# Score masks on ScalarE that take the eighth maximum itself as bias, and one VectorE operation for the exponential's bias in place of three on GpSimd

## The chip, the core and the metric

The kernel runs on one core of one Trainium2 chip. The metric is the time of one execution on the device in microseconds (us): 1217.75 as the median of three runs (1216.57 to 1219.38). Everything is computed in fp32, partly with operands split into two parts.

## The reference, cut to what matters

Attention over 4 batches and 8 heads, 576 positions, 64 channels, in which each row keeps only its 32 largest scores, and behind it two MLPs (512 to 2048 and back) over the 2304 tokens:

```python
scores = scale * np.matmul(q, k.transpose(0, 1, 3, 2))
kth = np.partition(scores, -top_k, axis=-1)[..., -top_k:-top_k + 1]      # top_k = 32
mask = scores >= kth
scores = np.where(mask, scores, -1000000000.0)
scores = scores - np.max(scores, axis=-1, keepdims=True)
attn = np.exp(scores)
attn = attn / (np.sum(attn, axis=-1, keepdims=True) + 1e-09)
x = np.matmul(attn, v)                # rows of all heads side by side: 2304 x 512
h = x @ w_in;  x = (h - np.tanh(h)) @ w_out
h = x @ w_in2; x = np.where(h > 0, h, np.exp(np.minimum(h, 0)) - 1) @ w_out2
```

## The kernel before

**Stages.** The 2304 tokens go through in six chunks of 384. Chunk 0's attention runs alone; from then on the MLPs of one chunk (two times 16 steps: a product to `h`, an activation, a gate `g`, a split of `g` into `gh` and `gl`, a second product) are interleaved with the attention of the next chunk. Behind the attention of chunk 5 only MLP steps are left. The weights come packed; in chunk 0 and during its MLPs they are unpacked by ScalarE (lines 186, 203), VectorE (line 189) and a split on ScalarE and GpSimd (line 148 and 149, tile `wp`).

**Attention.** A group is up to three tiles of 128 query rows by 576 scores (tile `s`, copied from PSUM by ScalarE, line 385). A group takes four rounds r = 0 to 3. In each round VectorE finds the eight largest values of each row (`find`, MAX8, line 406, into `vm`) and, in rounds 0 to 2, replaces them by a very low number (`drop`, MATCH_REPLACE8, line 420). The eighth value of round 3 is the row's 32nd largest score, the threshold. For most tiles VectorE then multiplies the exponential with the mask (line 427). For some it is ScalarE that makes the mask: `MASK_ACT = [3, 2, 1, 0, 0, 0]` tiles of each group in chunks 0, 1 and 2 (the last group of chunk 0, which is in a hurry, has none). These are 45 tiles in 23 groups: 7 groups with three tiles, 8 with two, 8 with one.

**The mask on ScalarE.** Prelu of `s - threshold` with the slope 3e38 for negative arguments (line 422), then the exponential of that with a bias that adds back the threshold and takes off the row's largest value (line 423). The first needs `nk`, the threshold negated, the second `b2` (named `b` in the profile), the scaled threshold plus `mb`. GpSimd makes both in three small operations (lines 412, 413, 414) of 1 to 3 columns. `mb` is the negated, scaled maximum, made by GpSimd in round 0 (line 408).

**Order.** Python code issues the work by ticks (four ticks to a group); a scheduler then sets the order of the instructions on each engine, and each engine works its queue strictly in that order, so a waiting instruction holds up all that stand behind it. TensorE's score products (lines 383, 384) use three PSUM banks, which ScalarE's copies (line 385) give back.

**GpSimd's other work** in the stretch that the change touches: the low halves of the splits, all by line 149 (`wp` 1024 columns, `kk` 576, `gl` and `xl` 384), `qs` (line 326), and `xun` (line 559), most of which read two tiles in SBUF.

Of the kernel before, what the change touches and what calls it, by code (L numbers as in the profile page):

```python
# [8 lines left out]
F32 = mybir.dt.float32  # L9
# [4 lines left out]
AF = mybir.ActivationFunctionType  # L14
ALU = mybir.AluOpType
# [3 lines left out]
P = 128  # L19
# [4 lines left out]
SCALE = 0.125  # L24
# [3 lines left out]
NF = DFF // P  # L28
FILL = -1.0e38

STEEP = 3.0e38


CHUNKS = [
# [72 lines left out]
def tile_topk_attention_two_mlps(  # L107
# [9 lines left out]
    nc = tc.nc  # L117

    def pool(name, bufs, space=None):
        kw = {} if space is None else {"space": space}  # L120
        return ctx.enter_context(tc.tile_pool(name=name, bufs=bufs, **kw))

    const = pool("const", 1)
    sb = pool("sb", 2)
# [108 lines left out]
    for ci, size in enumerate(SIZES):  # L233
        for p in range(NPAIR):
            row = []
            c0 = 0
            for b, q0, n in CHUNKS[ci]:
                for heads in ([[0], [1]] if n >= 256 else [[0, 1]]):
                    u = Unit()
# [18 lines left out]
            for us in cuts:  # L258
                g = Group()
# [11 lines left out]
    def hurried(u):  # L271

        return u.rush and u.last
# [113 lines left out]
    def topk_steps(g, r):  # L387

        k = len(g.tiles)
        if r == 0:  # L390
            g.vm = sb.tile([P, 4, 2, 8], F32, tag="vm", name=f"vm{g.id}")
            g.mb = sb.tile([P, 4], F32, tag="mb", name=f"mb{g.id}")
            g.sum = sb.tile([P, 4], F32, tag="sum", name=f"sum{g.id}", bufs=8)
            g.w = [sb.tile([P, S], F32, tag="w3", name=f"w3{g.id}_{j}", bufs=W_BUFS) for j in range(k)]
        if r == 1:
            for u in g.units:
                u.e = [sb.tile([P, S], F32, tag="e", name=f"e{u.id}_{t}", bufs=E_BUFS) for t in range(u.k)]

        by_act = 0 if g.rush and hurried(g.units[-1]) else min(k, MASK_ACT[g.units[0].ci])
        if r == 3 and by_act:  # L400
            g.nk = sb.tile([P, 4], F32, tag="nk", name=f"nk{g.id}")
            g.b2 = sb.tile([P, 4], F32, tag="b2", name=f"b2{g.id}")

        def find(j):
            u, t = g.tiles[j]
            nc.vector.max(g.vm[:, j, min(r, 1)], u.s[t] if r == 0 else g.w[j])  # L406
            if r == 0 and j == k - 1:
                nc.gpsimd.tensor_scalar_mul(g.mb[:, :k], g.vm[:, :k, 0, 0], -SCALE)
            if r == 1 and j >= by_act:
                nc.scalar.activation(u.e[t], u.s[t], AF.Exp, bias=g.mb[:, j : j + 1], scale=SCALE)  # L410
            if r == 3 and j == by_act - 1:
                nc.gpsimd.tensor_scalar_mul(g.nk[:, :by_act], g.vm[:, :by_act, 1, 7], -1.0)
                nc.gpsimd.tensor_scalar_mul(g.b2[:, :by_act], g.vm[:, :by_act, 1, 7], SCALE)
                nc.gpsimd.tensor_add(g.b2[:, :by_act], g.b2[:, :by_act], g.mb[:, :by_act])

        def drop(j):
            u, t = g.tiles[j]
            v = g.vm[:, j, min(r, 1)]
            if r < 3:
                nc.vector.match_replace(g.w[j], v, u.s[t] if r == 0 else g.w[j], FILL)  # L420
            elif j < by_act:
                nc.scalar.activation(u.e[t], u.s[t], AF.Prelu, bias=g.nk[:, j : j + 1], alpha=STEEP)
                nc.scalar.activation(  # L423
                    u.e[t], u.e[t], AF.Exp, bias=g.b2[:, j : j + 1], scale=SCALE, accum_out=g.sum[:, j : j + 1]
                )
            else:
                nc.vector.scalar_tensor_tensor(
                    u.e[t], u.s[t], v[:, 7:8], u.e[t], op0=ALU.is_ge, op1=ALU.mult, accum_out=g.sum[:, j : j + 1]
                )

        return [lambda j=j, d=d: d(j) for d in (find, drop) for j in range(k)]

    def transposed(g, blk):
# [297 lines left out]
    for tick in range(FIRST_TICK, n_ticks):  # L731
# [10 lines left out]
        for u in units:  # L742
            if hurried(u) and tick == 4 * u.g.at + 4:
# [4 lines left out]
                finish_pair(u)  # L748
        at, r = divmod(tick, 4)
        chain = topk_steps(groups[at], r) if 0 <= at < len(groups) else []  # L750
        todo = [step_parts(i) for i in at_tick.get(tick, ())]
        cuts = [len(chain) * j // (2 * max(1, len(todo))) for j in range(2 * max(1, len(todo)) + 1)]
# [60 lines left out]
```

## Time and profile before

| what | value |
|---|---|
| median of three runs | 1217.75 us |
| the profiled execution | 1221.19 us, of which the span of instructions is 1219.4 us |
| busy in the span: PE, DVE, ACT, POOL | 94%, 78%, 63%, 41% |
| granted TensorE clock, mean over the span | 0.972 |

PE is TensorE, PEld its weight loads, DVE VectorE, ACT ScalarE, POOL GpSimd. The shares of the whole span mix stages: the first 170 us are attention alone, then comes the interleaved stretch, and from 1050 us on the MLPs run alone. In the chain that ended last (it can be followed back to 451 us) PE has 58% of the span, ACT 2% and DVE 1%.

### The profile page before, as it was taken

What the parts mean: (1) busy time and instruction counts of PE and PEld (TensorE: products, weight loads), DVE (VectorE), ACT (ScalarE), POOL (GpSimd) and SP (SyncE); (2) the same over time, 40 slices, a digit from 0 to 9 for tenths busy, and PEclk for the clock granted to TensorE, in tenths of its full rate; (3) what the DMA queues carried; (4) which work ended last, traced back from release to release, by engine and by line L of the source; (5) the groups of instructions that cost most, each with busy time, mean ns of one, the idle gap of its engine ahead of it and who ended that gap; (6) DMA issues with size and microseconds to landing.
All of it is one profiled execution on the core that took longest, in us unless ns stands there. A gap on an engine that the chain in (4) does not pass through costs nothing.

```text
span 1219.4 us, 18848 instructions
## 1 busy us (share of the span) xinstructions
PE 1150.4 (94%) x6349; PEld 976.2 (80%) x6349; DVE 950.1 (78%) x1896; ACT 764.1 (63%) x1592; POOL 503.1 (41%) x557
## 2 busy tenths in 40 slices
PE   6477789998999999999999999999999999999998
PEld 3344478887887978898988988988988988898897
DVE  7899999998999999789888779898789996100111
ACT  4999978988975546474564666575555564432333
POOL 2345348666752323253524444434434413333221
PEclk9688899998999999999999999999999999999999
DMA  7999728984989985759886779988679875686572
GB/s 233 361 354 336 241 73 295 365 288 142 385 345 290 288 302 144 246 162 315 251 187 206 238 239 247 226 243 271 218 248 221 205 154 207 210 285 247 195 270 95
DMA packets 81328, 299.59 MB, mean 246 GB/s; under 512 B 18768, under 2 KB 36048, under 8 KB 51664
## 3 DMA queue, kind: packets, MB, share of 16 engines
q1 hardware_dynamic: 81232, 298.39, 76.8%
q8 instruction: 50, 0.82, 0.3%
q14 instruction: 46, 0.38, 0.1%
HBM read 252.97 MB, written 45.39 MB: 245 GB/s over the span
## 4 chain that ended last, share of the span: by engine, by line
PE 58%; ACT 2%; DVE 1%; POOL 0%; issue 0%; ACTq 0%; POOLq 0%; DVEq 0%
PE acc L613 24%; PE h L577 24%; PE av L470 3%; PE pt L448 3%; PE ps L383 2%; PE ps L384 2%; DVE vm L406 0%; ACT y L627 0%; DVE w L420 0%; ACT zh L632 0%; ACT e L410 0%; ACT ph L449 0%; ACT s L385 0%; POOL kk L149 0%; ACT t L583 0%
## 5 line engine op out<-in xcount | busy, mean ns | idle before, releaser
L149 POOL TENSOR_TENSOR gl<-g,gh 128x384 fp32r<-128x384 f32 x192 | 203.4, 1061 | 371.8 <-ACT gh L148 352.3
L406 DVE MAX8 vm<-w 128x8 f32<-128x576 f32 x432 | 315.8, 748 | 3.2
L613 PE MATMUL acc<-wt,gh 128*128 128x512 f32 x1002 | 267.2, 398 | 0.3 <-ACT gh L148 0.3
L420 DVE MATCH_REPLACE8 w<-vm,w 128x576 f32<-128x576 f32 x288 | 212.8, 740 | 0.0
L613 PEld LDWEIGHTS acc<-wt,gh 128*128 128x128 f32 x1002 | 183.7, 188 | 33.9 <-issue 2.7
L148 ACT ACTIVATE gh<-g 128x384 fp32r<-128x384 f32 x192 | 100.6, 526 | 83.8 <-DVE g L591 43.3
L591 DVE SCALAR_TENSOR_TENSOR g<-t,h 128x384 f32<-128x384 f32 x96 | 52.4, 545 | 127.8 <-ACT t L583 127.4
L577 PE MATMUL h<-zh,wt 128*128 128x384 f32 (+2 forms) x768 | 145.8, 326 | 2.4 <-ACT zh L632 1.2
L613 PE MATMUL acc<-wt,gl 128*128 128x512 f32 x501 | 146.4, 398 | 0.0
L577 PE MATMUL h<-xh,wt 128*128 128x384 f32 x664 | 140.0, 339 | 2.0 <-DVE g L591 1.2
L448 PE MATMUL pt<-ident,e 128*116 128x128 f32 (+1 forms) x720 | 117.8, 290 | 20.2 <-ACT e L423 8.3
L385 ACT ACTIVATE s<-ps 128x288 f32<-128x288 f32 (+1 forms) x272 | 106.8, 416 | 45.2 <-PE ps L384 36.6
L406 DVE MAX8 vm<-s 128x8 f32<-128x576 f32 x144 | 107.4, 751 | 34.6 <-ACT s L385 32.6
L577 PEld LDWEIGHTS h<-zh,wt 128*128 128x128 f32 x768 | 124.9, 190 | 8.8 <-ACT zh L632 2.4
L449 ACT ACTIVATE ph<-pt 116x384 f32<-116x384 f32 (+1 forms) x240 | 111.2, 500 | 30.0 <-PE pt L448 29.5
L448 PEld LDWEIGHTS pt<-ident,e 128*116 128x116 f32 (+1 forms) x720 | 90.4, 143 | 43.2 <-ACT e L423 11.4
L577 PEld LDWEIGHTS h<-xh,wt 128*128 128x128 f32 x664 | 116.2, 188 | 9.0 <-DVE g L591 1.5
L582 ACT ACTIVATE t<-h 128x384 f32<-128x384 f32 x96 | 46.7, 488 | 108.2 <-PE h L577 108.0
L613 PEld LDWEIGHTS acc<-wt,gl 128*128 128x128 f32 x501 | 92.1, 188 | 18.5
L420 DVE MATCH_REPLACE8 w<-vm,s 128x576 f32<-128x576 f32 x144 | 106.6, 741 | 0.0
L580 ACT ACTIVATE t<-h 128x384 f32<-128x384 f32 x96 | 47.0, 491 | 90.9 <-PE h L577 90.8
L596 DVE TENSOR_TENSOR g<-h,t 128x384 f32<-128x384 f32 x76 | 41.4, 546 | 72.0 <-ACT t L580 71.5
(82 smaller groups left out, 1958.3 us busy)
## 6 DMA issues: line engine op xcount, KB each, us to landing
wt<-w SPq DMA_DIRECT2D x167, 1024.0 KB, 6.0
wr<-in_w_dram SPq DMA_DIRECT2D x32, 1024.0 KB, 8.9
w<-wp SPq DMA_DIRECT2D x32, 1024.0 KB, 8.4
kraw<-in_kT_dram SPq DMA_DIRECT2D x96, 144.0 KB, 5.4
vraw<-in_vL_dram SPq DMA_DIRECT2D x64, 160.0 KB, 5.2
sd<-sp SPq DMA_DIRECT2D x24, 288.0 KB, 5.8
s<-sd SPq DMA_DIRECT2D x24, 288.0 KB, 8.9
qraw<-in_qT_dram SPq DMA_DIRECT2D x64, 96.0 KB, 5.6
```

The lines of the kernel that those rows point to most:

```text
L148: nc.scalar.activation(hi, src, copy)
L149: return nc.gpsimd.tensor_sub(lo, src, f(hi))
L385: nc.scalar.activation(s[lo:hi, cs], pt[lo:hi, :HS], copy)
L406: nc.vector.max(g.vm[:, j, min(r, 1)], u.s[t] if r == 0 else g.w[j])
L420: nc.vector.match_replace(g.w[j], v, u.s[t] if r == 0 else g.w[j], FILL)
L448: nc.tensor.transpose(pt[:kn, j * P : j * P + P], v.e[t][:, k0 : k0 + kn], ident)
L449: nc.scalar.activation(g.ph[:kn, blk, :nq], pt[:kn, :nq], copy)
L577: nc.tensor.matmul(h[:, cs], wv[:, wi, kt], xs[:, kt, cs], start=(a == 0), stop=(a == len(jobs) - 1))
L580: nc.scalar.activation(t, h, AF.Tanh)
L582: nc.scalar.activation(t, h, AF.Relu, scale=-1.0)
L591: nc.vector.scalar_tensor_tensor(g, t, -1.0, h, op0=ALU.add, op1=ALU.max)
L613: nc.tensor.matmul(acc[ci, m][t], gx[:, t * P : t * P + P], wt[:, wi], start=(ft == 0 and k == 0), stop=(ft == NF - 1 and k == 2),)
```

## The change

`nk` and its operation go. ScalarE's Prelu now computes threshold minus score, with the eighth maximum in `vm` itself as bias and the scale -1; a score that is kept gives a value of zero or below, which the slope 2^-100 makes tiny, and one that is dropped stays positive. The exponential undoes both by the scale -0.125 times 2^100. `b2` is made by one VectorE operation, issued directly behind the MAX8 of the group's last ScalarE tile. GpSimd's three operations per group go. In the changed file the lines behind the deleted one are lower by one (406 becomes 405, 422 becomes 421), and the new operation has line 411.

```diff
--- before.py
+++ after.py
@@ -28,7 +28,7 @@
 NF = DFF // P
 FILL = -1.0e38
 
-STEEP = 3.0e38
+FLAT = 2.0**-100
 
 
 CHUNKS = [
@@ -398,7 +398,6 @@
 
         by_act = 0 if g.rush and hurried(g.units[-1]) else min(k, MASK_ACT[g.units[0].ci])
         if r == 3 and by_act:
-            g.nk = sb.tile([P, 4], F32, tag="nk", name=f"nk{g.id}")
             g.b2 = sb.tile([P, 4], F32, tag="b2", name=f"b2{g.id}")
 
         def find(j):
@@ -409,9 +408,9 @@
             if r == 1 and j >= by_act:
                 nc.scalar.activation(u.e[t], u.s[t], AF.Exp, bias=g.mb[:, j : j + 1], scale=SCALE)
             if r == 3 and j == by_act - 1:
-                nc.gpsimd.tensor_scalar_mul(g.nk[:, :by_act], g.vm[:, :by_act, 1, 7], -1.0)
-                nc.gpsimd.tensor_scalar_mul(g.b2[:, :by_act], g.vm[:, :by_act, 1, 7], SCALE)
-                nc.gpsimd.tensor_add(g.b2[:, :by_act], g.b2[:, :by_act], g.mb[:, :by_act])
+                nc.vector.scalar_tensor_tensor(
+                    g.b2[:, :by_act], g.vm[:, :by_act, 1, 7], SCALE, g.mb[:, :by_act], op0=ALU.mult, op1=ALU.add
+                )
 
         def drop(j):
             u, t = g.tiles[j]
@@ -419,9 +418,9 @@
             if r < 3:
                 nc.vector.match_replace(g.w[j], v, u.s[t] if r == 0 else g.w[j], FILL)
             elif j < by_act:
-                nc.scalar.activation(u.e[t], u.s[t], AF.Prelu, bias=g.nk[:, j : j + 1], alpha=STEEP)
+                nc.scalar.activation(u.e[t], u.s[t], AF.Prelu, bias=v[:, 7:8], scale=-1.0, alpha=FLAT)
                 nc.scalar.activation(
-                    u.e[t], u.e[t], AF.Exp, bias=g.b2[:, j : j + 1], scale=SCALE, accum_out=g.sum[:, j : j + 1]
+                    u.e[t], u.e[t], AF.Exp, bias=g.b2[:, j : j + 1], scale=-SCALE / FLAT, accum_out=g.sum[:, j : j + 1]
                 )
             else:
                 nc.vector.scalar_tensor_tensor(
```

The scheduler sets a new order on every engine. ScalarE around 192 us of the profile before (the mask of group 0_1_0_1_0_0: batch 0, chunk 1, pair 0; `e` is the exponential's tile), before:

```order
L148 ACTIVATE kk_2_0_384_0_0_2072<-kraw_2_0_384_0_0_1849 128x576
L449 ACTIVATE ph_0_1_0_0_384_0_1680<-pt_0_1_0_0_384_0_3_1751 116x384
L148 ACTIVATE wp_8_1776<-wf_8_1772 128x2x512
L580 ACTIVATE t_0_4_1808<-h_0_4_1795 128x384
L449 ACTIVATE ph_0_1_0_0_384_0_1680<-pt_0_1_0_0_384_0_4_1756 112x384
L422 ACTIVATE e_0_1_0_0_0_1632<-s_0_1_0_0_0_1424,nk_0_1_0_1_0_0_1793 128x576
L422 ACTIVATE e_0_1_0_0_1_1633<-s_0_1_0_0_1_1453,nk_0_1_0_1_0_0_1793 128x576
L148 ACTIVATE wp_9_1842<-wf_9_1838 128x2x512
L186 ACTIVATE wr_10_1907<-wr_10_1907 128x1024
L203 ACTIVATE wr_10_1907<-wr_10_1907 128x1024
L580 ACTIVATE t_0_5_1874<-h_0_5_1861 128x384
L385 ACTIVATE s_1_1_0_0_0_1881<-ps_1_1_0_0_0_0_0_1882 128x288
```

and now:

```order
L148 ACTIVATE kk_2_0_384_0_0_2045<-kraw_2_0_384_0_0_1822 128x576
L421 ACTIVATE e_0_1_0_0_0_1608<-s_0_1_0_0_0_1403,vm_0_1_0_1_0_0_1543 128x576
L448 ACTIVATE ph_0_1_0_0_384_0_1656<-pt_0_1_0_0_384_0_3_1727 116x384
L448 ACTIVATE ph_0_1_0_0_384_0_1656<-pt_0_1_0_0_384_0_4_1732 112x384
L579 ACTIVATE t_0_4_1783<-h_0_4_1770 128x384
L148 ACTIVATE wp_8_1752<-wf_8_1748 128x2x512
L421 ACTIVATE e_0_1_0_0_1_1609<-s_0_1_0_0_1_1432,vm_0_1_0_1_0_0_1543 128x576
L409 ACTIVATE e_1_0_384_0_2_1892<-s_1_0_384_0_2_1710,mb_1_1_1_0_384_0_1829 128x576
L579 ACTIVATE t_0_5_1847<-h_0_5_1834 128x384
L385 ACTIVATE s_1_1_0_0_0_1854<-ps_1_1_0_0_0_0_0_1855 128x288
L148 ACTIVATE gh_0_4_1793<-g_0_4_1791 128x384
L422 ACTIVATE e_0_1_0_0_0_1608,sum_0_1_0_1_0_0_1545<-e_0_1_0_0_0_1608,b_0_1_0_1_0_0_1769 128x576
```

The two Prelus have moved up, the first over a copy to `ph` and ahead of `wp`; the weight unpacking (`wr`) that stood between them and the copy of `s_1_1_0_0_0` stands behind it now.

VectorE at the same group (`w` is what is left of the scores), before:

```order
L406 MAX vm_0_1_0_1_0_0_1567<-w_0_1_0_1_0_0_1_1571 128x8
L406 MAX vm_1_1_1_0_384_0_1855<-s_1_0_384_0_2_1734 128x8
L420 MATCH_REPLACE w_0_1_0_1_0_0_2_1572<-vm_0_1_0_1_0_0_1567,w_0_1_0_1_0_0_2_1572 128x576
L406 MAX vm_1_1_1_0_384_0_1855<-w_1_1_1_0_384_0_0_1858 128x8
L189 SCALAR_TENSOR_TENSOR wf_9_1838<-wr_9_1836 128x1024
L420 MATCH_REPLACE w_1_1_1_0_384_0_1_1859<-vm_1_1_1_0_384_0_1855,s_1_0_384_0_1_1655 128x576
L596 TENSOR_TENSOR g_0_4_1818<-h_0_4_1795,t_0_4_1808 128x384
L406 MAX vm_0_1_0_1_0_0_1567<-w_0_1_0_1_0_0_2_1572 128x8
L420 MATCH_REPLACE w_1_1_1_0_384_0_0_1858<-vm_1_1_1_0_384_0_1855,w_1_1_1_0_384_0_0_1858 128x576
```

and now:

```order
L405 MAX vm_0_1_0_1_0_0_1543<-w_0_1_0_1_0_0_1_1547 128x8
L405 MAX vm_0_1_0_1_0_0_1543<-w_0_1_0_1_0_0_2_1548 128x8
L405 MAX vm_1_1_1_0_384_0_1828<-w_1_1_1_0_384_0_0_1831 128x8
L189 SCALAR_TENSOR_TENSOR wf_9_1811<-wr_9_1809 128x1024
L595 TENSOR_TENSOR g_0_4_1791<-h_0_4_1770,t_0_4_1783 128x384
L411 SCALAR_TENSOR_TENSOR b_0_1_0_1_0_0_1769<-vm_0_1_0_1_0_0_1543,mb_0_1_0_1_0_0_1544 128x2
L419 MATCH_REPLACE w_1_1_1_0_384_0_1_1832<-vm_1_1_1_0_384_0_1828,s_1_0_384_0_1_1631 128x576
L426 SCALAR_TENSOR_TENSOR e_0_1_0_0_2_1610,sum_0_1_0_1_0_0_1545<-s_0_1_0_0_2_1465,vm_0_1_0_1_0_0_1543,e_0_1_0_0_2_1610 128x576
```

The first row of both is the MAX8 that gives the threshold of the group's second tile. The new operation (tile `b`) stands behind the gate `g_0_4`, with four instructions between it and that MAX8; before, nothing of its kind stood on VectorE.

ScalarE where chunk 0 goes from its first MLP to the second (`zh` is the second one's input; `t` the activations of its first steps), before:

```order
L484 ACTIVATE xun_1_2747<-av_1_192_2749 128x192
L148 ACTIVATE xh_2163<-xun_1_2747 128x384
L385 ACTIVATE s_3_0_384_0_0_2823<-ps_3_0_384_0_0_0_0_2824 128x288
L186 ACTIVATE wr_8_3002<-wr_8_3002 128x1024
L385 ACTIVATE s_3_0_384_0_0_2823<-ps_3_0_384_0_0_1_0_2828 128x288
L203 ACTIVATE wr_8_3002<-wr_8_3002 128x1024
L422 ACTIVATE e_2_1_0_0_0_2862<-s_2_1_0_0_0_2456,nk_2_1_2_1_0_0_3025 128x576
L422 ACTIVATE e_2_1_0_0_1_2863<-s_2_1_0_0_1_2507,nk_2_1_2_1_0_0_3025 128x576
L582 ACTIVATE t_1_0_2713<-h_1_0_2688 128x384
L423 ACTIVATE e_2_1_0_0_0_2862,sum_2_1_2_1_0_0_2786<-e_2_1_0_0_0_2862,b_2_1_2_1_0_0_3026 128x576
L582 ACTIVATE t_1_1_2815<-h_1_1_2790 128x384
L385 ACTIVATE s_3_0_384_0_1_2886<-ps_3_0_384_0_1_0_0_2887 64x288
```

and now:

```order
L483 ACTIVATE xun_1_2711<-av_1_192_2713 128x192
L421 ACTIVATE e_2_1_0_0_1_2827<-s_2_1_0_0_1_2474,vm_2_1_2_1_0_0_2748 128x576
L148 ACTIVATE xh_2133<-xun_1_2711 128x384
L385 ACTIVATE s_3_0_384_0_0_2787<-ps_3_0_384_0_0_0_0_2788 128x288
L422 ACTIVATE e_2_1_0_0_0_2826,sum_2_1_2_1_0_0_2750<-e_2_1_0_0_0_2826,b_2_1_2_1_0_0_2989 128x576
L422 ACTIVATE e_2_1_0_0_1_2827,sum_2_1_2_1_0_0_2750<-e_2_1_0_0_1_2827,b_2_1_2_1_0_0_2989 128x576
L186 ACTIVATE wr_8_2966<-wr_8_2966 128x1024
L203 ACTIVATE wr_8_2966<-wr_8_2966 128x1024
L581 ACTIVATE t_1_0_2677<-h_1_0_2652 128x384
L581 ACTIVATE t_1_1_2779<-h_1_1_2754 128x384
L385 ACTIVATE s_3_0_384_0_0_2787<-ps_3_0_384_0_0_1_0_2792 128x288
```

The second Prelu has moved ahead of `xh` (the first one stands two rows above the piece, ahead of both copies to `xun`); the second copy to `s_3_0_384_0_0`, the fifth row before, is the last one now, behind both exponentials, both `wr` and two `t`.

## Rows read from the trace of the kernel before

**Rows 1.** Windows: us; busy us (instructions) by engine, PE clock, DMA share, GB/s

```profile
50.00:169.00 119.00, 91.89 (x385) 58.48 (x385) 116.28 (x230) 112.49 (x229) 51.38 (x65) 0.83 0.80 281
169.00:345.00 176.00, 166.03 (x998) 145.26 (x999) 166.61 (x305) 153.61 (x297) 121.92 (x112) 0.97 0.79 284
345.00:480.00 135.00, 132.16 (x763) 110.73 (x762) 133.51 (x280) 74.54 (x153) 44.67 (x70) 1.00 0.85 266
480.00:1050.00 570.00, 567.29 (x3299) 498.23 (x3299) 478.06 (x977) 333.50 (x742) 220.54 (x239) 1.00 0.79 227
```

**Rows 2.** Waits of PE, 170 to 500 us: total us, times, longest

```profile
PE ps L383 <- ACT s L385: 5.1, 3, 2.3
...
PE h L577 <- DVE g L591: 2.7, 3, 1.2
```

**Rows 3.** Timeline, VectorE, 167 us: start, duration, engine, line, operation, tiles

```profile
167.07 1.74 DVE L556 TENSOR_TENSOR xl<-xun,xh 128x384 fp32r<-128x384 f32 x1
```

**Rows 4.** Groups by line: busy us, mean ns; idle before, releaser

```profile
L149 POOL TENSOR_TENSOR gl<-g,gh 128x384 fp32r<-128x384 f32 x192 | 203.4, 1061 | 371.8 <-ACT gh L148 352.3 <-issue 13.1 <-PE ps L384 3.2
...
L149 POOL TENSOR_TENSOR wp<-wf,wp 128x1024 fp32r<-128x1024 f32 x32 | 77.9, 2438 | 25.4 <-ACT wp L148 23.8 <-issue 1.6
...
L410 ACT ACTIVATE e<-s,mb 128x576 f32<-128x576 f32 x99 | 70.6, 772 | 15.1 <-POOL mb L408 15.0
...
L423 ACT ACTIVATE e<-e,b 128x576 f32<-128x576 f32 x45 | 35.2, 790 | 1.7 <-POOL b L414 1.2
...
L422 ACT ACTIVATE e<-s,nk 128x576 f32<-128x576 f32 x45 | 33.2, 793 | 11.4 <-POOL nk L412 8.2 <-DMA vraw<-in_vL_dram 3.2
```

**Rows 5.** Timeline, VectorE, 62 us

```profile
62.43 0.18 DVE L501 RECIPROCAL r<-r 128x6 f32<-128x6 f32 x1
62.53 2.04 DVE L406 MAX8 vm<-w 128x8 f32<-128x576 f32 x3
```

**Rows 6.** Timeline, VectorE and GpSimd, 146 to 150 us

```profile
146.85 0.81 DVE L427 SCALAR_TENSOR_TENSOR e<-s,vm,e 128x576 f32<-128x576 f32 x1
...
148.92 1.51 DVE L427 SCALAR_TENSOR_TENSOR e<-s,vm,e 128x576 f32<-128x576 f32 x1
...
148.82 1.00 POOL L559 TENSOR_TENSOR xun<-xun,rs 128x384 f32<-128x384 f32 x1 [1.86 <-ACT xun L484]
```

**Rows 7.** What GpSimd's line 412 waited for: us, times

```profile
  DVE vm L406: 21.5, 11
```

**Rows 8.** Timeline, GpSimd and VectorE, 118 to 122 us

```profile
118.16 2.39 POOL L149 TENSOR_TENSOR wp<-wf,wp 128x1024 fp32r<-128x1024 f32 x1
120.51 0.23 POOL L412 TENSOR_SCALAR nk<-vm 128x3 f32<-128x3 f32 x1
120.71 0.23 POOL L413 TENSOR_SCALAR b<-vm 128x3 f32<-128x3 f32 x1
...
120.92 1.23 DVE L189 SCALAR_TENSOR_TENSOR wf<-wr 128x1024 uint32<-128x1024 uint32 x1 [1.27 <-POOL b L413]
```

**Rows 9.** Timeline, VectorE, GpSimd, ScalarE and TensorE, 189 to 201 us

```profile
189.13 0.74 DVE L406 MAX8 vm<-w 128x8 f32<-128x576 f32 x1
...
192.64 2.31 POOL L149 TENSOR_TENSOR kk<-kraw,kk 128x576 fp32r<-128x576 f32 x1
194.93 0.21 POOL L412 TENSOR_SCALAR nk<-vm 128x2 f32<-128x2 f32 x1
...
195.18 1.45 ACT L422 ACTIVATE e<-s,nk 128x576 f32<-128x576 f32 x2 [3.18 <-POOL nk L412]
...
199.90 0.68 ACT L385 ACTIVATE s<-ps 128x288 f32<-128x288 f32 x2
...
200.33 0.40 PE L383 MATMUL ps<-kk,qs 128*128 128x288 f32 x1 [2.25 <-ACT s L385]
```

**Rows 10.** Timeline, TensorE, 277 us

```profile
277.74 0.61 PE L383 MATMUL ps<-kk,qs 128*128 128x288 f32 x1 [2.28 <-ACT s L385]
```

**Rows 11.** Window 270 to 290 us, columns as in Rows 1

```profile
270.00:290.00 20.00, 17.29 (x98) 15.77 (x98) 17.75 (x35) 17.60 (x36) 7.88 (x13) 0.83 0.47 172
```

## The prediction

> **What bounds the kernel now.** I read the windows by stretch first, then TensorE's waits, then the timelines at the places found.
>
> [Rows 1]: from 50 to 169 us VectorE is busy 116.3 of 119 us, ScalarE 112.5, TensorE waits for them. This is chunk 0's attention, and VectorE sets its length; its last piece is the low half of chunk 0's `x`, which ends at 167.07 + 1.74 = 168.8 us [rows 3] and lets the first MLP begin. From 169 to 345 us (chunk 1's attention beside chunk 0's MLPs) TensorE has 166.0 of 176 us and VectorE 166.6: both are at their limit, and GpSimd is busier than anywhere else (121.9). From 345 to 480 us (chunk 2's) TensorE has 132.2 of 135, VectorE 133.5. Behind 480 us TensorE has 567.3 of 570: its work there is fixed, so what is lost or won ahead of it arrives at the end one for one. All 23 groups that the change touches lie ahead of 480 us: 7, 8 and 8 in the three stretches. In the interleaved part TensorE's waits name both engines [rows 2]: ScalarE's copy to `s` 5.1 us in three waits, VectorE's gate 2.7 us in three.
>
> **The change part by part.**
>
> *ScalarE's work.* 45 Prelus and 45 exponentials stay, on the same 128x576 tiles, with a scale and a column as bias. Forms with and without a scale differ by 0.02 us (772, 790 and 793 ns) [rows 4], so 45 x 0.02 = 0.9 us of ScalarE either way at most. I take 0.
>
> *VectorE's new operation, its slot.* No row shows an operation of three columns with two inputs. The nearest is the reciprocal of six columns: 0.18 us long, but the next MAX8 starts 0.10 us behind its start [rows 5]. Nothing that follows the new operation on VectorE needs its result, so I take 0.10: 0.7 us in the first stretch, 0.8 in each of the others, 2.3 in all. The bounds are 0 (it falls where VectorE would have waited) and 23 x 0.18 = 4.1.
>
> *VectorE's new operation, its wait.* The mask multiplication of line 427 reads two SBUF tiles, as the new operation does (`vm` and `mb`). It takes 0.81 us, and 1.51 us where GpSimd runs `xun` from 148.82 to 149.82 us: it ends 0.6 us behind GpSimd's end [rows 6]. So it stood still while GpSimd read. The new operation can be caught in this way; then all VectorE work behind it waits too, gates included, though it computes for a moment only. Lower bound 0: in 11 of 23 groups GpSimd sat idle waiting for that very MAX8 [rows 7]. Upper bound by chance arrival: GpSimd's busy share is 0.43, 0.69 and 0.33 [rows 1], and the rest of the instruction met is on average half of it, between 0.5 us (`gl`) and 1.2 us (`wp`) [rows 4]. I estimate 0.8, 0.9 and 0.55 us for the three mixtures: 0.35, 0.6 and 0.2 us each time, 7 x 0.35 + 8 x 0.6 + 8 x 0.2 = 8.9 us. I take half, because of the 11 of 23: 1.2, 2.4 and 0.8 us.
>
> The Trainium skill (SBUF — State Buffer, section "Who interferes with whom") has a rule that speaks against this edit: a VectorE instruction with two SBUF inputs contends with a GpSimd instruction that reads SBUF, and the one that comes second stands still until the other is done. The two durations of [rows 6] agree. By that rule at every chance meeting the whole upper bound falls due; it is the first rival below.
>
> *GpSimd's three operations go.* They held VectorE up as well: at 119.65 us the unpacking of line 189 began to wait, the split `wp` ended at 118.16 + 2.39 = 120.55 us, and VectorE started only at 120.92, behind `nk` and the first half of `b` [rows 8]. That is 0.4 us back, in the first stretch. What else GpSimd gains costs or brings nothing by itself: no TensorE wait names it in [rows 2].
>
> *ScalarE's wait for the threshold.* In chunk 1 the threshold was there at 189.13 + 0.74 = 189.87 us, but GpSimd was busy up to a 2.31 us split of `kk` and made `nk` at 194.93 us; ScalarE stood for 3.18 us. Behind the Prelus came `wp`, two `wr` and a `t`, so that the copy to `s` came at 199.90 us, and TensorE stood for 2.25 us until a PSUM bank was free [rows 9]. Now the Prelus need only `vm`, they stand earlier, and the `wr` stand behind the copy. I take 2.2 us off TensorE's path; the bounds are 0 (the next wait takes its place) and 2.25. ScalarE's other waits for `nk`, 8.2 - 3.2 = 5.0 us [rows 4], I count as nothing: of TensorE's 5.1 us of waits for copies [rows 2] this place has 2.25 and the turn from the first to the second MLP, at 277.74 us [rows 10], 2.28, where ScalarE was not waiting for `nk`.
>
> *The sum.* First stretch, where VectorE is the path, in full: 0.7 + 1.2 - 0.4 = +1.5. Second: VectorE gets 0.8 + 2.4 = 3.2 us; it has 176 - 166.6 = 9.4 us of its own idle time and TensorE waits for its gates only now and then, so half: +1.6. Third: 0.8 + 0.8 = 1.6, half by the same argument: +0.8. ScalarE's wait: -2.2. Together +1.7 us. The profiled execution took 1221.19 us, 1.8 more than its span and 3.4 more than the median of the runs; the sum is a difference, so I add it to the median: 1217.75 + 1.7 = 1219.4 us.
>
> **The rivals.**
>
> *GpSimd holds VectorE at full price (slower).* Place: chunk 1, where GpSimd is busy 122 of 176 us. Each new operation costs 0.1 + 0.6 us, 5.6 in place of the 1.6 I let through, because VectorE's idle time there lies elsewhere; and 7 x 0.35 = 2.45 in place of 1.2 in chunk 0. That is 1.7 + 4.0 + 1.3 = +7.0 us, 1224.8. For it: GpSimd no longer stops to wait for the MAX8, so it takes up the next split and is more often in the middle of one. Against it: the 11 of 23, and two TensorE waits that were ScalarE's. It decides from a mean wait of about 0.4 us per operation in chunk 1 on, where the sum passes +2.4.
>
> *ScalarE's freedom clears the second stall too (faster).* At 277.74 us TensorE had stood for 2.28 us [rows 10], and the granted clock over 270 to 290 us is 0.83 [rows 11]: of 20 us, 0.17 x 20 = 3.4 us were lost at the lower level, 1.2 GHz, right behind that wait. In the new order the two Prelus stand ahead of the copies to `xun` and of `xh`, where ScalarE waited anyway. If that wait shrinks enough for the clock to stay up, 2.28 + 3.4 = 5.7 us go: 1.7 - 5.7 = -4.0, 1213.8. Against it: the second copy to `s` now stands behind both exponentials, two `wr` and two `t`.
>
> *A new wait of the same kind (slower).* Every queue is ordered anew, and TensorE stands at its limit in the middle stretches. One new wait of 2.3 us with its 3.4 us at the lower clock costs 5.7: 1219.4 + 5.7 = 1225.1. Nothing in the profile of before points to its place.
>
> That the change does not do what it says is excluded by the new order: GpSimd's three operations are not in it, and VectorE's one is.
>
> **How the numbers follow.** My forecast 0.35, the first rival 0.23, the second 0.32, the third 0.10. A measurement of this kernel can tell about 0.2%, 2.4 us. So slower 0.23 + 0.10 = 0.33, same 0.35, faster 0.32. The likeliest case's own range is 1215.5 to 1220.1. The cases on both sides hold much of the chance, so the range reaches nearly to all of them: at the low end the second rival with a third of VectorE's 3.9 us (1.5 + 1.6 + 0.8) hidden as well, 1213.8 - 1.3 = 1212.5; at the high end the third rival, 1225.1, rounded to 1225.5.
>
> **What would show it.** Right: 23 new instructions on VectorE of 0.1 to 0.2 us with some of 1 us and more, and, at each long one, a GpSimd split that ends with it; the low half of `x` for chunk 0 (line 555) ending 1 to 2 us later than 168.8; no ScalarE wait ahead of line 421 that names GpSimd, and no TensorE wait near 200 us. The forecast is wrong if the new instructions are all short (then 3 to 4 us of the sum go), if VectorE's busy time from 169 to 345 us grows by far more than 3 us, or if the granted clock in that stretch leaves its 0.97 in either direction.

## The result: 1232.5 us, slower than before, and the profile after

The changed kernel took 1232.51 us as the median of four runs, beside 1217.16 for the kernel before on the same chip: a ratio of 1.0133, with a 95% interval of 1.0102 to 1.0163. The forecast was 1219.4 us and its range ended at 1225.5, so the change is slower than any case that was priced. The granted clock is 0.974 (0.972 before), so the clock is not what differs over the whole span.

The same four windows of the changed kernel, columns as in [rows 1]:

```profile
50.00:169.00 119.00, 89.24 (x382) 56.65 (x383) 118.97 (x238) 110.77 (x223) 47.18 (x46) 0.86 0.78 274
169.00:345.00 176.00, 160.76 (x959) 138.80 (x957) 170.44 (x306) 152.17 (x290) 115.83 (x87) 0.97 0.80 282
345.00:480.00 135.00, 129.33 (x745) 107.64 (x745) 130.08 (x281) 71.66 (x152) 35.06 (x43) 1.00 0.82 253
480.00:1050.00 570.00, 568.04 (x3298) 500.66 (x3297) 482.90 (x987) 333.48 (x744) 227.62 (x242) 1.00 0.77 227
```

TensorE got less done in each of the first three windows: it was 2.7, 5.3 and 2.8 us less busy than in [rows 1], with 3, 39 and 18 instructions fewer. From 480 us on it is full as before. So the loss lies ahead of 480 us and comes through to the end, as the prediction's first part said.

The new operation, as the view of its line gives it (duration minimum, median, maximum in ns):

```profile
L411 DVE SCALAR_TENSOR_TENSOR b<-vm,mb x23: 130/291/1485, 38.3 to 482.7; 128x2 f32<-128x2 f32 x8, 128x1 f32<-128x1 f32 x8, 128x3 f32<-128x3 f32 x7
```

All 23 together take 11.2 us. Eleven take 0.13 to 0.15 us; in the trace the other twelve begin while GpSimd is in the middle of an operation and end 0.01 to 0.02 us behind that operation's end. One of them, with the GpSimd split beside it (start, duration):

```profile
83.27 2.38 POOL L149 TENSOR_TENSOR wp<-wf,wp 128x1024 fp32r<-128x1024 f32 x1 [0.49 <-ACT wp L148]
```

```profile
84.43 1.23 DVE L411 SCALAR_TENSOR_TENSOR b<-vm,mb 128x3 f32<-128x3 f32 x1
```

The split ends at 85.65 us and the operation of three columns at 85.66: it computed for about 0.14 us and stood for the rest.

The low half of chunk 0's `x`, which [rows 3] has at 167.07 us for 1.74 us, and the place of [rows 9] on ScalarE:

```profile
167.27 0.53 DVE L555 TENSOR_TENSOR xl<-xun,xh 128x384 fp32r<-128x384 f32 x1
```

```profile
191.50 0.76 ACT L421 ACTIVATE e<-s,vm 128x576 f32<-128x576 f32 x1
```

Chunk 0 is handed over at 167.8 us, 1.0 earlier than in the trace of before (that execution was 4.0 us above the median of its runs, this one 0.3 below), and the mask runs at 191.50 without the 3.18 us wait for GpSimd. What TensorE waits for from 170 to 500 us (total, times, longest), beside [rows 2]:

```profile
PE ps L383 <- ACT s L385: 5.8, 6, 1.6
PE h L576 <- DVE g L595: 3.3, 3, 2.3
PE pt L447 <- ACT s L385: 2.1, 5, 0.8
PE pt L447 <- ACT ph L448: 1.8, 1, 1.8
PE h L576 <- DVE g L590: 1.8, 1, 1.8
PE pt L447 <- ACT e L422: 1.7, 1, 1.7
PE h L576 <- DVE zl L632: 1.3, 1, 1.3
```

The wait of 2.25 us at 200.33 is gone. In its stead stand many of 0.8 to 2.3 us, each at another place and for another engine. No single row accounts for 15 us.

### The profile page after: what moved, and what is told of

It reads as the page before. It is cut to its first block, busy times and chain, and to the rows that moved or that the text cites. A ratio compares the mean times of both kernels' runs of the same rounds, so it can differ in the third digit from the quotient of the medians.

```text
span 1230.4 us, 18812 instructions
## 1 busy us (share of the span) xinstructions
PE 1150.4 (93%) x6349; PEld 974.7 (79%) x6349; DVE 961.0 (78%) x1919; ACT 765.0 (62%) x1592; POOL 492.4 (40%) x488
## 4 chain that ended last, share of the span: by engine, by line
PE 70%; DVE 19%; ACT 6%; DMA 3%; issue 2%; POOL 1%; SPq 0%; ACTq 0%; DVEq 0%; POOLq 0%
PE h L576 28%; PE acc L612 28%; DVE vm L405 8%; DVE w L419 6%; PE av L469 4%; PE pt L447 4%; DVE wf L189 2%; PE ps L383 2%; PE ps L384 2%; DMA s<-sd 1%; DVE e L426 1%; PE ps L371 1%; DMA wr<-in_w_dram 1%; ACT s L385 1%; PE pp L371 1%
## 5 line engine op out<-in xcount | busy, mean ns | idle before, releaser
L149 POOL TENSOR_TENSOR gl<-g,gh 128x384 fp32r<-128x384 f32 x192 | 209.4, 1093 | 386.3 <-ACT gh L148 354.7
L447 PE MATMUL pt<-ident,e 128*116 128x128 f32 (+1 forms) x720 | 112.4, 284 | 28.4 <-ACT e L422 12.4
L447 PEld LDWEIGHTS pt<-ident,e 128*116 128x116 f32 (+1 forms) x720 | 87.0, 139 | 49.8 <-ACT e L422 15.9
```

Source lines behind the costliest of these rows:

```text
L149: return nc.gpsimd.tensor_sub(lo, src, f(hi))
L447: nc.tensor.transpose(pt[:kn, j * P : j * P + P], v.e[t][:, k0 : k0 + kn], ident)
```

## Experiments

Three moments in the trace place the loss: the hand-off (chunk 0's last `xl` ends), turn 1 and turn 2 (the last `zl` of chunk 1 and of chunk 2 ends, where that chunk goes from its first MLP to the second). From turn 2 to the end of the span every kernel below takes nearly the same time. Each row is one execution, and executions of one kernel lie some us apart (f10: 1214.5 to 1220.1 us), so a difference of 1 or 2 us between two rows is not read.

| profiled execution | hand-off | turn 1 | turn 2 | end of span less turn 2 |
|---|---|---|---|---|
| before | 168.8 | 459.1 | 631.9 | 587.5 |
| after | 167.8 | 472.2 | 643.7 | 586.7 |
| f3_gp_b2_in_before_order | 168.1 | 457.3 | 630.1 | 586.2 |
| f10_reduce_in_before_order | 167.4 | 459.0 | 631.9 | 586.2 |
| f1_after_in_before_order | 168.9 | 464.8 | 637.6 | 586.2 |
| f6_gp_b2_in_after_order | 164.4 | 465.9 | 637.4 | 586.2 |
| g4_reduce_in_after_order | 161.9 | 463.2 | 634.7 | 586.7 |
| g7_reduce_turn_first | 161.3 | 457.8 | 634.7 | 586.7 |
| g6_masks_first | 169.0 | 466.8 | 645.9 | 586.3 |

### Other operations, each in the order that the scheduler gave it

**e1_no_b2**: no bias for the exponential at all. A row's bias is a factor that cancels in the normalisation.

```diff
-                nc.vector.scalar_tensor_tensor(
-                    g.b2[:, :by_act], g.vm[:, :by_act, 1, 7], SCALE, g.mb[:, :by_act], op0=ALU.mult, op1=ALU.add
-                )
...
-                    u.e[t], u.e[t], AF.Exp, bias=g.b2[:, j : j + 1], scale=-SCALE / FLAT, ...
+                    u.e[t], u.e[t], AF.Exp, scale=-SCALE / FLAT, ...
```

> The changed kernel without any operation for the exponential's bias (the bias is 0: the row's largest value is not taken off, which cancels in the division by the sum). Neither VectorE nor GpSimd has an operation for it. If the new operation's standing behind GpSimd is the cause, VectorE's busy time falls by about the 11 us of the 23 operations and the time goes back to 1215 to 1221 us. If the new order of the queues is the cause, the time may lie anywhere from 1215 to 1235, and VectorE's busy time alone does not tell.

Measured: 1222.91 us, ratio 1.0042 [1.0027, 1.0057].

**e2_one_input**: VectorE's operation with one input in the SBUF.

```diff
+                nc.vector.tensor_scalar_mul(g.b2[:, :by_act], g.vm[:, :by_act, 1, 7], SCALE)
```

> The changed kernel with the VectorE operation in the same place and of the same size, but with one input (the threshold times the scale; the row's largest value is not taken off, which cancels in the division by the sum). The order of all queues stays that of the changed kernel. If the second input in SBUF makes it stand behind GpSimd, the 23 operations fall from 11.2 us to 2.5 to 3.5 us, none is longer than 0.2 us, and the time falls by 5 to 8 us, to 1224 to 1228. If the new order is the cause, the time stays at 1231 to 1234.

Measured: 1232.65 us, 1.0121 [1.0104, 1.0137].

```profile
L411 DVE TENSOR_SCALAR b<-vm x23: 134/158/1487, 36.8 to 481.3; 128x2 f32<-128x2 f32 x8, 128x1 f32<-128x1 f32 x8, 128x3 f32<-128x3 f32 x7
```

The longest is 1.49 us here too, eight take 0.6 us or more and end 0.03 us behind a GpSimd operation, and the 23 sum to 10.0 us: taking the second input away did not take the waits away.

**e3_gp_b2**: the masks take `vm`, and GpSimd still makes `b2`, in its two operations; only `nk` goes.

> Half of the change: the masks take the eighth maximum itself, nk goes, but the exponential's bias is made by GpSimd's two operations as before. VectorE gets nothing. If VectorE's new operation is the cause, the time is that of before or below, 1212 to 1219. If losing the wait for nk (a new order, other meetings of GpSimd and VectorE) is the cause, it is 1225 or more.

Measured: 1222.96 us, 1.0044 [1.0029, 1.0059].

**e4_before_dve_b2**: `nk` and the masks as before, `b2` by the new VectorE operation.

> The other half: nk stays on GpSimd and the masks use it; only the exponential's bias is made by VectorE's one operation. If VectorE's new operation is the cause, its 23 instances take 8 to 12 us and the time is 1226 to 1235. If the order is the cause, the operation may be as long and the time still 1215 to 1222.

Measured: 1230.33 us, 1.0103 [1.0086, 1.012].

All four are slower than before, e1 and e3 too, which have no new operation on any engine. Every edit gives another order of all queues than that of before (in the traces some 900 to 1400 of TensorE's 6349 instructions stand elsewhere), so none of these runs differs from before by one change alone. Only e2 has the order of the changed kernel, but for a few instructions.

### The same order, other operations; the same operations, another order

To part the two, the queues were tied to an order taken from another kernel's program: each instruction may only be issued behind the one that precedes it in a table. In the traces of f1 and f3 every engine's instructions then stand as in before, and in those of f6 and g4 as in the changed kernel, apart from the operations that the edit takes out or puts in. What the tying itself costs was not measured by a kernel tied to its own order; f3, f4 and f10 at 1215.9 to 1218.4 us leave little room for it.

```diff
         tile_topk_attention_two_mlps(tc, *args)
+        pin(tc, nc.cur_bb.bb.instructions)
...
+        for a, b in zip(queue, queue[1:]):
+            tc.add_manual_dep(
+                b, a.name, mybir.DependencyInfo(mybir.DependencyClass.NoSync, mybir.DependencyReason.DATA), reason="pin"
+            )
```

**f1_after_in_before_order**, the changed kernel in the order of the one before:

> The changed kernel's instructions, unaltered, but every engine's queue is tied to the order that it has in the kernel before; VectorE's new operation stands where the last of GpSimd's three stood. If the new order is what costs the time: 1214 to 1221 us, the kernel before's 1217.4 with the direct price or gain of the operations themselves. If the new operation on VectorE and its meetings with GpSimd cost it: 1228 to 1234, as the changed kernel.

Measured: 1225.38 us, 1.0067 [1.0053, 1.0081]. Between the two theories' numbers: both are at work.

**f3_gp_b2_in_before_order**, the operations of e3:

> The instructions of the run in which the masks take the eighth maximum and GpSimd still makes the exponential's bias in two operations (1222.96 us in the order that the scheduler gave it), with every queue tied to the order of the kernel before. Order theory: 1214 to 1218 us, 5 to 8 below the same instructions in their own order, and at or a little under the kernel before, since ScalarE's masks no longer wait for GpSimd. If instructions set the time and not their order: 1223 again.

Measured: 1215.92 us, 0.9991 [0.998, 1.0002].

**f6_gp_b2_in_after_order**, the operations of e3 in the changed kernel's order:

> The same instructions as the run before this one, with every queue tied to the order of the changed kernel: there is no operation of the change on VectorE at all. Order theory: 1228 to 1233 us, as slow as the changed kernel. Operation theory: 1223 or less, since what was to cost the time is gone.

Measured: 1224.81 us, 1.0061 [1.0048, 1.0075]: less than the order theory said, more than f3 by 8.9 us with not an instruction changed.

**n1_nk_last**, the kernel before with one line moved:

```diff
-                nc.gpsimd.tensor_scalar_mul(g.nk[:, :by_act], g.vm[:, :by_act, 1, 7], -1.0)
                 nc.gpsimd.tensor_scalar_mul(g.b2[:, :by_act], g.vm[:, :by_act, 1, 7], SCALE)
                 nc.gpsimd.tensor_add(g.b2[:, :by_act], g.b2[:, :by_act], g.mb[:, :by_act])
+                nc.gpsimd.tensor_scalar_mul(g.nk[:, :by_act], g.vm[:, :by_act, 1, 7], -1.0)
```

> The kernel before with its three GpSimd operations written in another sequence (the mask's bias after the exponential's): the same instructions on the same engines, nothing for VectorE. The order of all queues comes out otherwise, some 1240 rows on TensorE. Order theory: it differs from 1217.4 us by several us, most likely upward, 1220 to 1231, because the order of the kernel before is the best of the six seen. Operation theory: 1217 to 1219, at most the wait for one more short GpSimd operation on some of the 23 masks.

Measured: 1223.67 us, 1.0054 [1.0038, 1.007]. The same instructions on the same engines, 6.6 us slower through the order alone.

**f4_no_b2_in_before_order**, the operations of e1:

> No operation for the exponential's bias on any engine (it is 0; a factor of a row cancels in the normalisation), the masks take the eighth maximum, every queue in the order of the kernel before. Against the changed kernel in that order (1225.4 us) it lacks only VectorE's 23 operations, so the difference is their whole price: 8 to 11 us by the pair measured before (1225.4 against 1215.9), which gives 1214 to 1217. If the masks' form or ScalarE's part of the change had cost something: 1219 or more.

Measured: 1215.9 us, 0.998 [0.9968, 0.9992], the one version whose interval lies below the kernel before.

**f8_one_input_in_before_order**, the operation of e2:

> VectorE's operation as a tensor_scalar with one input in the SBUF, every queue in the order of the kernel before. In the first run with this form 10 of 23 still took 0.6 to 1.5 us, each ending within 0.04 us of the GpSimd operation that ran when it began. If both forms wait for the running GpSimd operation: 1222 to 1226 us, near the 1225.4 of the two-input form. If only the second input waits: 1217 to 1219, 23 operations at 0.15 us.

Measured: 1222.7 us, 1.0036 [1.0024, 1.0049]. (In the trace of e2, the first run with this form, eight operations take 0.6 us or more and not ten.)

**f10_reduce_in_before_order**:

```diff
+                nc.vector.tensor_reduce(
+                    g.b2[:, :by_act], g.vm[:, :by_act, 1, 7:8], op=ALU.max, axis=mybir.AxisListType.X
+                )
```

> VectorE's operation as a tensor_reduce over one element (the bias is then the eighth maximum unscaled; a factor of a row cancels), at the same place, every queue in the order of the kernel before. If the price is the wait for GpSimd and this form is free of it: the 23 operations take 0.1 to 0.2 us each, none near 1 us, and the time is 1216 to 1219. If an operation at this place costs by standing in VectorE's queue (its wait for the maxima, what it pushes back): 1223 to 1226 as the other forms.

Measured: 1218.42 us, 0.9999 [0.9987, 1.001]. The three forms at the same place in the same order, f1, f8 and f10:

```profile
L411 DVE SCALAR_TENSOR_TENSOR b<-vm,mb x23: 139/171/1386, 39.7 to 482.2; 128x2 f32<-128x2 f32 x8, 128x1 f32<-128x1 f32 x8, 128x3 f32<-128x3 f32 x7
```

```profile
L411 DVE TENSOR_SCALAR b<-vm x23: 131/158/1412, 39.7 to 479.4; 128x2 f32<-128x2 f32 x8, 128x1 f32<-128x1 f32 x8, 128x3 f32<-128x3 f32 x7
```

```profile
L411 DVE TENSOR_REDUCE b<-vm x23: 130/142/164, 40.0 to 476.5; 128x2 f32<-128x2 f32 x8, 128x1 f32<-128x1 f32 x8, 128x3 f32<-128x3 f32 x7
```

The reduction never takes over 0.16 us. The first of f10 and the GpSimd split that it met show that it had the same chance to wait:

```profile
38.87 2.37 POOL L149 TENSOR_TENSOR wp<-wf,wp 128x1024 fp32r<-128x1024 f32 x1 [2.14 <-ACT wp L148]
...
39.98 0.15 DVE L411 TENSOR_REDUCE b<-vm 128x3 f32<-128x3 f32 x1
```

It ended at 40.13 us, with 1.1 us of the split to go. So the wait is shown to be what the other two forms pay for: without waits the 23 reductions sum to 3.3 us, those of f8 to 10.3 and those of f1 to 13.3.

**f9_after_8_s_bufs**, in the changed order:

```diff
-S_BUFS = 7
+S_BUFS = 8
-Y_BUFS = 3
+Y_BUFS = 2
```

> The changed kernel with its own order tied, eight score buffers in place of seven and, to make room, two y buffers in place of three. If the order's cost is VectorE's wait for the reload of parked scores, which is issued when a score buffer comes free (4.9 us of waits in three places between 400 and 441 us): these waits go and the time is 1226 to 1229. If those waits are hidden behind TensorE anyway: 1231 to 1234.

Measured: 1263.64 us, 1.0372 [1.0354, 1.039]. It tells nothing of the reload: VectorE still waits for it, 7.5 us, and the buffer that was given up to make room costs far more. ScalarE's copies `o` and TensorE behind them wait for the stores:

```profile
L645 ACT ACTIVATE o<-acc x18: 590/597/661, 378.4 to 1256.9; 128x512 f32<-128x512 f32 x18
...
  DMA out_dram<-o: 25.9, 5
```

### Where the order costs

**g1_before_first** and **g3_before_to_turn** splice the two orders at the hand-off and at turn 1.

> The changed kernel's instructions; every queue in the order of the kernel before up to chunk 0's hand-off (its last xl), from there in the changed kernel's own order. If the order costs its 7 us behind the hand-off, where TensorE's queue has 33 more instructions ahead of chunk 1's turn (2074 in place of 2041): 1230 to 1234, as the changed kernel. If it costs them in the first stretch: 1224 to 1227.

> The changed kernel's instructions; every queue in the order of the kernel before up to chunk 1's turn (its last zl), from there in the changed kernel's own order. If the order costs its time ahead of that turn: 1224 to 1227, as with the whole order of the kernel before (1225.4). If behind it: 1230 to 1234.

Measured: g1 1233.19 us, 1.0133 [1.0108, 1.0157]; g3 1233.11, 1.0128 [1.0104, 1.0152]. g1 shows that the first stretch is not the place. g3 does as well as f1 up to turn 1 (464.8 us in both) and then takes 181.0 us to turn 2 where f1 takes 172.8; but its seam is a new order of its own, with a granted clock of 0.85 from 470 to 480 us and 0.81 from 480 to 490, where both parents have 1.00.

**g4_reduce_in_after_order** takes the wait alone out of the changed kernel.

> The changed kernel in its own order with VectorE's operation as the tensor_reduce over one element, which took 0.13 to 0.16 us each time. If the two causes add up: 1224 to 1227, the changed kernel's 1232.5 without the 7.0 us that this form saved in the order of the kernel before. If in this order the wait is hidden, as the one-input form's 1232.65 might suggest: 1230 to 1233.

Measured: 1223.32 us, 1.0055 [1.0034, 1.0076], 9.2 us below the changed kernel: the two causes add up.

**g5_turn_first**, **g6_masks_first** and **g7_reduce_turn_first** move a few instructions at turn 1 (some 30 in g5 and g7, fewer in g6).

> The changed kernel in its own order, but at chunk 1's turn the instructions of the turn stand first: TensorE's 12 yt transposes and 16 h products ahead of 10 av, 4 ps and 6 pt, ScalarE's three zh right behind its three y copies and ahead of the mask, VectorE's three zl ahead of its b operation. In the changed kernel y was copied by 461.3 us and zh only began at 467.1, behind the mask, which waited 2.1 us for VectorE. If that is what the order costs: 1226 to 1229 us, 4 to 6 below the changed kernel. If the order's cost is spread over the queues: 1231 to 1233.

> The changed kernel's instructions in the order of the kernel before (1225.4 us), but at chunk 1's turn one mask of ScalarE stands ahead of the three zh copies (and two ph copies), and VectorE's three zl behind the maxima that this mask waits for: ten instructions moved by a few places. In that order the mask ran at 462.9 and zh at 457.6 us. If the turn's place behind a mask is what costs: zh some 5 to 6 us later and 1228 to 1232. If not: 1225 to 1226.

> Both causes taken out of the changed kernel: its own order with the turn first, and VectorE's operation in the form that doesn't wait for GpSimd (1223.3 us without the first of these). If the account is complete: 1217 to 1220, as the kernel before. If something else of the order costs: 1222 to 1224.

Measured: g5 1231.2 us, 1.0109 [1.0088, 1.0129]; g6 1232.87, 1.0128 [1.0111, 1.0144]; g7 1223.39, 1.005 [1.0036, 1.0064]. g6 came out as the theory said, g5 and g7 did not. In g6 the mask that was moved waits for its maxima and makes everything behind it late, on ScalarE and then on TensorE:

```profile
463.66 0.78 ACT L421 ACTIVATE e<-s,vm 128x576 f32<-128x576 f32 x1 [2.96 <-DVE vm L405]
464.34 1.55 ACT L631 ACTIVATE zh<-yt 128x512 fp32r<-128x512 f32 x3
```

```profile
465.46 3.78 PE L576 MATMUL h<-zh,wt 128*128 128x256 f32 x16 [5.40 <-ACT zh L631]
...
460.00:470.00 10.00, 4.60 (x22) 4.54 (x22) 9.33 (x21) 3.02 (x7) 0.23 (x1) 0.68 0.40 124
```

In f1 the same 16 products ran at once:

```profile
458.79 2.15 PE L576 MATMUL h<-zh,wt 128*128 128x256 f32 x16
```

TensorE stood for 5.4 us, and those products then took 3.78 us in place of 2.15: the granted clock is 0.68 over these 10 us, so part of them ran at the lower level, 1.2 GHz. Price: 7.5 us, from one mask (and VectorE's maxima for it) ahead of the turn. But the reverse move in the changed order brought only 1.3 us (g5; 2.9 by the ratios, about the width of the intervals) and nothing without the wait (g7): turn 1 came 5.4 us earlier in g7 than in g4, and turn 2 at 634.7 us in both. So turn 1 is a place where order can cost that much, and is not the place where the changed order loses it.

What is left is read from f3 and f6, which have the same instructions. From hand-off to turn 2 in three windows and their sum, first f3, then f6:

```profile
168.10:270.30 102.20, 96.54 (x585) 84.65 (x584) 99.29 (x190) 87.33 (x171) 71.17 (x63) 0.97 0.77 280
270.30:457.30 187.00, 181.90 (x1058) 155.15 (x1058) 179.84 (x352) 130.12 (x254) 84.66 (x95) 0.98 0.85 293
457.30:630.10 172.80, 172.29 (x971) 150.74 (x968) 150.02 (x308) 98.65 (x220) 64.95 (x73) 1.00 0.72 217
```

```profile
164.40:263.90 99.50, 95.03 (x581) 82.70 (x580) 96.10 (x190) 88.21 (x173) 70.38 (x63) 0.98 0.81 285
263.90:465.90 202.00, 189.91 (x1084) 160.35 (x1082) 187.39 (x367) 131.22 (x258) 88.54 (x95) 0.97 0.85 274
465.90:637.40 171.50, 170.10 (x953) 148.98 (x952) 143.43 (x291) 94.93 (x214) 67.37 (x73) 1.00 0.75 217
```

f6 takes 473.0 us for this where f3 takes 462.0. TensorE's idle time is 473.0 - 455.0 = 18.0 us against 462.0 - 450.7 = 11.3, so 6.7 of the 11.0 us are waits, and they lie between turn 0 (the end of the first window) and turn 1: 12.1 us there against 5.1. VectorE's own waits from 345 to 480 us name one large wait that f3 does not have in that view at all:

```profile
DVE vm L405 <- DMA s<-sd: 5.4, 3, 2.6
```

This is the reload of chunk 2's parked scores; the changed kernel has 4.9 us of it, f1 0.8, the kernel before 1.5. It goes with this slow order in every trace that has it (4.9 to 6.9 us in after, e2, f6, g1, g4, g5 and g7), but not with slow orders as such: e1, e3 and n1, some 7 us slower than their instructions in the order of before, have 0, 0.5 and 1.4 us of it. That it causes the loss is not shown: f9, which was to test it, failed by its other edit. The remaining 4.3 us of the 11.0 are in TensorE's busy time. Some 2.2 of them are work that f3 does ahead of the hand-off (TensorE is busy for 119.4 us there, in f6 for 117.2); the rest is not assigned.

The traces of the other kernels agree on the place. From turn 0 to turn 1 the six kernels with the order of before (before, f1, f3, f4, f8, f10) take 187.0 to 192.5 us, the five with the changed kernel's order behind the hand-off (after, e2, f6, g1, g4) 200.4 to 202.9. Other orders lose elsewhere: e1 and e3 take 190.1 and 188.3 us there, but 110.7 and 111.1 from the hand-off to turn 0, where f4 and f3 take 101.7 and 102.2.

## Why the prediction was wrong

**The account.** Put in a row, the ratios telescope: before to f3 (`nk` gone) -0.0009, f3 to f10 (an operation on VectorE that does not wait) +0.0008, f10 to f1 (its wait) +0.0068, f1 to after (the order) +0.0066; together +0.0133. On 1217.2 us that is -1.1, +1.0, +8.3 and +8.0 us, in all 16.2 (the ratios are not exactly those of the medians, which lie 15.4 apart). Each step carries an uncertainty of 0.002 to 0.003, some 2 to 4 us.

**What was right.** What is lost ahead of turn 2 arrives one for one (586.2 to 587.5 us from there to the end in every kernel of the table). ScalarE's wait for the threshold goes, and with it the stall of 2.25 us at 200 us; f3, where this is the only gain, stands 1.1 us below before (the interval reaches from -2.4 to +0.2), in place of the 2.2 that were counted. The new operations are 0.13 to 0.15 us long except where a GpSimd operation ends with them. VectorE's busy time from 169 to 345 us grew by 3.8 us and the clock there kept its 0.97. One of the signs named did not come: chunk 0's last `xl` ended 1.0 us earlier, not 1 to 2 later. With executions some us apart this decides little, and the new order does other work ahead of it (in f1, with the old order, it ends at 168.9).

**The term that was mis-sized: VectorE's operation and its wait.** The prediction had 2.3 us of slots and at most 8.9 us of waits, and took 4.4 of the 8.9. The 23 operations of the changed kernel last 11.2 us. Without a wait they last about 0.14 us each, 3.2 in all, so 8.0 us are waits, nearly twice what was taken. (That 2.3 + 8.9 is 11.2 as well is chance: where nothing waits, VectorE's next instruction starts there 0.06 to 0.07 us behind the operation's start, so the 23 slots are some 1.4 us.) The 8.9 was not an upper bound either: the waits come to 10.1 us in f1 and 13.7 in e4, whose 23 operations sum to 13.3 and 16.9. It was the size to expect.

The step that failed is "I take half, because of the 11 of 23": the busy shares that it was worked out from already hold the times at which GpSimd is idle, so the 11 of 23 [rows 7] were taken off twice. Those shares give 7 x 0.43 + 8 x 0.69 + 8 x 0.33 = 11.2 meetings; in the changed kernel twelve operations began in the middle of a GpSimd operation and eleven did not. The rule of the Trainium skill that was weighed there (SBUF — State Buffer, "Who interferes with whom") bore out at each of the twelve. It also says that `tensor_scalar` can enter modes that use the shared ports, and that `tensor_reduce` on trn2 never contends; f8 and f10 agree, with 1.41 and 0.16 us as the longest.

**Where it arrives.** The prediction let it through in full in the first stretch and by half in the second and third. In the order of before it was the other way about. From f3 to f1 the hand-off moves by only 0.8 us though 5.0 us of the operations lie ahead of it (2 to 3 us, if f3's execution, 2.2 us above the median of its runs, lost that ahead of the hand-off). From the hand-off to turn 1 the time grows by 6.7 us on 8.0 us of operations. Ahead of the hand-off VectorE had waits that took part of it up, as that of f3, gone in f1:

```profile
121.53 1.23 DVE L189 SCALAR_TENSOR_TENSOR wf<-wr 128x1024 uint32<-128x1024 uint32 x1 [1.81 <-ACT wr L203]
```

In the order of the changed kernel the first stretch does pay: from g4 to after the hand-off moves by 5.9 us, with 3.1 us more of operations ahead of it.

In the interleaved stretch VectorE's lateness soon is TensorE's. Waits of TensorE from 169 to 345 us for the gate of line 594 in f3 and of line 595 in f1, the same instruction:

```profile
PE h L575 <- DVE g L594: 1.4, 1, 1.4
```

```profile
PE h L576 <- DVE g L595: 4.8, 3, 2.0
```

VectorE's 9.4 us of idle time there gave little cover. The prediction's ground for the half, that TensorE waits for the gates only now and then, was read from 2.7 us in three waits [rows 2]; the same view of before has a further row between the two that are shown, so that the gates make 5.4 us, more than ScalarE's copies:

```profile
PE h L577 <- DVE g L596: 2.7, 1, 2.7
```

The first rival, the full price, said 1224.8; in the order of before this came out at 1225.4. It was the right mechanism with too small a chance. That the two times lie so close is in part luck: the rival counted 2.2 us of gain for ScalarE where f3 shows 1.1, and f1's operations sum to 13.3 us.

**The term that was missing: the order.** The third rival had the kind ("every queue is ordered anew"), a price of 5.7 us and a chance of 0.10, because nothing in the profile of before points to its place. Six pairs hold the instructions and change the order:

| operations | order of before | another order | difference | by the ratios |
|---|---|---|---|---|
| of before | 1217.1 | 1223.7 (n1, own) | 6.6 | 6.6 |
| of the change | 1225.4 (f1) | 1232.5 (after, own) | 7.1 | 8.0 |
| one input | 1222.7 (f8) | 1232.7 (e2, own) | 10.0 | 10.3 |
| reduction | 1218.4 (f10) | 1223.3 (g4, of after) | 4.9 | 6.8 |
| GpSimd's two | 1215.9 (f3) | 1223.0 (e3, own), 1224.8 (f6, of after) | 7.1, 8.9 | 6.5, 8.5 |
| none | 1215.9 (f4) | 1222.9 (e1, own) | 7.0 | 7.5 |

The last column takes each time against the runs of the kernel before that stood beside it, on 1217.2 us. The other orders are four (n1's, e1's, e3's and the changed kernel's, which e2, f6 and g4 have), and each is 6 to 10 us worse than that of before. So this price belongs to no operation of the change: an edit that swaps lines on GpSimd pays it as well. And the first two rivals were taken as alternatives to the third, though an order and a wait can both be lost, which is why the range ended below the time: the first rival's 1224.8 and the third's 5.7 would have made 1230.5.

**What stays open.** Which rows between turn 0 and turn 1 make the changed order worse; turn 1 alone does not (g5, g7), the first stretch does not (g1). That the kernel before in the changed order would be as slow was not run: there the first mask of a group stands ahead of the last maximum that `nk` needs, so its instructions do not fit that order.

## What to carry to other kernels

Where a scheduler orders the queues, two versions that differ by one operation differ by their whole order as well: tie both to one order before pricing the operation, and change the order alone to see its share. A short VectorE operation beside a busy GpSimd costs the rest of the GpSimd operation that it meets; multiply the busy share by the mean rest, and take nothing off that for idle moments (here 8.9 us by that, 8.0 in the changed kernel, 7 to 14 in other orders), or use a form that does not wait. Here the version without the operation, in the order of before, gains 0.2% (f4).

## What the runs showed of the hardware

A `tensor_scalar` with one input and two or three columns waits for GpSimd as a two-input operation does, and its end waits also for a fill that only writes. In e2 (first the GpSimd split and the fill, then the operation):

```profile
68.60 2.37 POOL L149 TENSOR_TENSOR wp<-wf,wp 128x1024 fp32r<-128x1024 f32 x1 [0.53 <-ACT wp L148]
...
70.66 0.68 DVE L411 TENSOR_SCALAR b<-vm 128x3 f32<-128x3 f32 x1
70.90 0.42 POOL L294 MEMSET qw<- 64x384 f32 x1
```

The split ended at 70.97 us, the fill at 71.32 and the operation at 71.34; VectorE's next MAX8 began at 70.91 all the same. Two operations of f8, at 70.82 and 85.02 us, ended behind a fill in the same way. The two-input form did not: where a fill followed the split, at 70.80 and 84.71 us in f1, it ended 0.02 to 0.03 us behind the split and 0.3 us ahead of the fill's end.

With one column the one-input form did not wait, in three of three meetings (one in f8, two in e2), where the two-input form did (0.87 us at 352.15 in f1). In f8:

```profile
348.55 2.38 POOL L149 TENSOR_TENSOR wp<-wf,wp 128x1024 fp32r<-128x1024 f32 x1 [0.19 <-ACT wp L148]
...
350.07 0.14 DVE L411 TENSOR_SCALAR b<-vm 128x1 f32<-128x1 f32 x1
```

A `tensor_reduce` of the same columns took 0.13 to 0.16 us at all 23 places of f10, eight of them in the middle of a GpSimd operation (one of these a fill).
